# Moving convolution operations between the blocks of a spilled round in a two-layer MLP kernel

## The chip, the cores and the metric

The kernel runs on one core of one Trainium2 chip. The metric is the device time of that core in microseconds (us), from runs on the chip. A profile of one execution stands beside the times: it names the engines PE (TensorE matmuls), PEld (TensorE weight loads), DVE (VectorE), ACT (ScalarE), POOL (GpSimd) and SP (SyncE, which here only issues DMAs).

## What is computed

The reference takes x of shape (8, 4096, 192), that is 32768 tokens of width 192. A causal convolution of 7 taps runs along each sequence; the taps are a softmax over `weight`, one set for each of 8 groups of channels. Then a two-layer MLP follows: h = x @ w_in with 2048 hidden units, g = s * relu(h)^2 + b, and out = g @ w_out, with 192 outputs.

```python
out = np.einsum('hk,bskhg->bshg', w, x_unf)      # 7 taps, w = softmax(weight)
h = x @ w_in
r = np.maximum(h, 0.0)
g = s * (r * r) + b
return (g @ w_out).astype(np.float32)
```

## The kernel before

**Tokens and steps.** The 32768 tokens are 32 super-blocks of 1024, each of two blocks of 512. A block has 8 steps, one for each pair of 128-wide slices of the hidden layer (`NPAIR` = 8). A step computes its pair's hidden values on PE (`first`, line 545), applies relu and square on ACT (lines 573 and 581), splits the square into a high and a low part on DVE (line 583 makes `qh`, line 587 makes `ql`), and two steps later adds the pair's share to the output rows 0 to 127 on PE (`second`, line 763). These output rows are the "A" part.

**Rounds.** The other 64 output rows, the "B" part, are not summed step by step. The squares `q` are kept, and from the third super-block on they are summed in rounds of 48 steps, that is of six blocks (`ROUNDS`). SBUF has a ring of 12 tiles for kept squares (`RING`, `room_for`), each of two steps, so a round's last three blocks stay on the chip and its first three are written to DRAM (`send`, line 602) and read back (`call_back`, line 612, 1 MB a tile, four tiles a block). `blocks(k)` returns these two lists as `near` and `far_off`. This text calls the near blocks n0, n1, n2 and the far ones f0, f1, f2; `batch` sums them in this order, in the second step of the next round. There are ten rounds: nine are summed by `batch`, the last by `last_batch`, which the change does not touch.

**A block's sum and its eviction.** `second_B` (line 782) adds a block's eight pairs into two PSUM tiles, `acc1` and `acc2`; `banks()` takes them from the pool `ps_o`, which has two buffers of each name. So a block's sum can begin when the block two places ahead of it has been evicted: f0 waits for n1, f1 for n2, f2 for f0. `evict_B` is one ACT activation (line 795) and three DVE operations (line 799), which together combine the four quarters into an output tile, and then a DMA (line 800).

**Convolution.** The convolution of the tokens to come runs on DVE in small pieces, drawn from one stream (`pieces`): seven tap operations a block (line 194 the first, line 196 the others), then a cast on ACT (line 232), a subtraction on DVE (line 225) and two DMAs that swap halves (lines 208 and 209). `convolve(k)` draws up to k pieces and puts them where it is called; it stops when a block has its seven taps, or when the stream says "gated", which means that it is as far ahead as it may be. In `batch`, `WINDOW` = 5 pieces are drawn for each block.

**Order.** DVE, ACT, PE and SP each carry out their instructions in the order in which the program writes them (`in_order`). A piece of convolution that is written ahead of an eviction therefore runs ahead of it, on DVE and, for the cast, on ACT. Some transfers written inside a round's sums are held (`put_off`) and released together by `let_go`, after the eviction of f1. `meanwhile` in `batch` is the relu, square and split of the round's first two steps.

Of the kernel before, what the change touches and what calls it, by code (L numbers as in the profile page):

```python
# [33 lines left out]
WINDOW = 5  # L34
# [13 lines left out]
def conv_attention_then_squared_relu_mlp(  # L48
# [78 lines left out]
    @contextmanager  # L127
    def in_order(*engines):

        traced = nc.cur_bb.bb.instructions  # L130
        start = len(traced)
        yield
        for e in engines:
            mine = [i for i in traced[start:] if i.engine == e.engine]
            for before, i in zip(mine, mine[1:]):
                tc.add_manual_dep(
                    i,
                    before.name,
                    mybir.DependencyInfo(
                        mybir.DependencyClass.NoSync, mybir.DependencyReason.DATA  # L140
                    ),
                    reason="in_order",
                )
# [4 lines left out]
    def put_off(transfer):  # L148
        if holding[0]:
            later.append(transfer)  # L150
        else:
            transfer()

    def let_go():
        holding[0] = False
        for transfer in later[-1:] + later[:-1]:
            transfer()
        later.clear()
# [435 lines left out]
    def place(block):  # L594
        return block // 2, block % 2
# [12 lines left out]
    def call_back(block):  # L608

        for k in range(NPAIR // 2):  # L610
            room = room_for(F32)
            nc.sync.dma_start(room.rearrange("p a b c -> p (a b c)"), away[block][:, k])
            for i in range(2):
                kept[*place(block), 2 * k + i] = room[:, i]
        del away[block]
# [5 lines left out]
    def blocks(k):  # L621

        z = (16 * OLD + sum(ROUNDS[: k + 1])) // NPAIR
        y = z - 2 * RING // NPAIR
        return list(range(y, z)), list(range(z - ROUNDS[k] // NPAIR, y))
# [18 lines left out]
    def banks():  # L644
        return [ps_o.tile([P, BLK], F32, name=f"acc{k}") for k in (1, 2)]
# [9 lines left out]
    def out_tile(name):  # L655
        return outs[:, room.index(name), :]
# [119 lines left out]
    def second_B(n, j, accs):  # L776

        for p in range(NPAIR):
            q = kept.pop((n, j, p))
            for r in (slice(0, HB), slice(HB, P)):  # L780
                for i in range(2):
                    nc.tensor.matmul(  # L782
                        accs[r.start // HB][i * DB : (i + 1) * DB], WB[r, p, i, :], q[r, i, :],
                        start=p == 0, stop=p == NPAIR - 1, skip_group_check=True,
                    )
        return accs
# [3 lines left out]
    def evict_B(n, j, accs):  # L790

        t0 = n * SUP + j * BLK
        oB = out_tile(("oB", "oB2", "oC", "oC2", "oA", "oA2")[turn[0] % 6])[0:DB]
        turn[0] += 1
        nc.scalar.activation(  # L795
            oB, accs[0][DB:P], AF.Identity, scale=sb[DB:P], bias=bias[DB:P, 1:2]
        )
        for a in (accs[0][0:DB], accs[1][0:DB], accs[1][DB:P]):
            nc.vector.scalar_tensor_tensor(oB, a, sb[0:DB], oB, op0=ALU.mult, op1=ALU.add)  # L799
        put_off(lambda: nc.sync.dma_start(outT[P:D, t0 : t0 + BLK], oB))  # L800
# [80 lines left out]
    def convolve(k):  # L881

        k += owed[0]
        owed[0] = 0
        while k > 0:
            said = next(stream, "over")
            if said in ("over", "gated"):
                return
            k -= 1
            burst[0] = k > 0  # L890
            if said == "tapped":
                owed[0] = k
                return
# [43 lines left out]
    def batch(k, meanwhile):  # L937

        near, far_off = blocks(k)
        inputs[0] = nc.sync  # L940
        with in_order(nc.sync):
            call_back(far_off[0])
            turn[0] = 0
            for block in near + far_off:
                a = second_B(*place(block), banks())
                if block == near[0]:
                    evict_B(*place(block), a)
                    meanwhile()
                    for away_block in far_off[1:]:
                        call_back(away_block)  # L950
                convolve(WINDOW)
                if block != near[0]:
                    evict_B(*place(block), a)
                if block == far_off[-2]:
                    let_go()
            convolve(0)
        inputs[0] = nc.scalar
# [28 lines left out]
    def step(n, j, p):  # L986
# [18 lines left out]
        if edge == 1:  # L1005
            second(*queue.pop(0))

            def puts():
                *at, before = waiting.pop()
                put(*at, squares(before, nc.vector.tensor_copy))  # L1010
                put(n, j, p, squares(h, nc.vector.tensor_copy))

            batch(k - 1, puts)
            return
# [89 lines left out]
```

## Time and profile before

| what | value |
|---|---|
| median of 3 runs (2245.11, 2246.98, 2247.1) | 2246.98 us |
| time of the profiled execution | 2247.28 us |
| its span, from the first instruction to the last | 2245.5 us |
| PE busy | 2220.7 us (99%) |
| PEld busy | 1612.3 us (72%) |
| DVE busy | 1668.6 us (74%) |
| ACT busy | 1297.8 us (58%) |
| mean granted TensorE clock | 0.999 of full speed |

The execution lasts 1.78 us longer than its span. Busy time is the share in which an engine has an instruction running; PE's is pipelined, and an end of a matmul is modelled, so the time that PE loses is better read from the starts of its instructions. A wait in the profile names the instruction that came last before a waiting one could start.

### The profile page before, as it was taken

How to read it: one execution, taken by the hardware profiler on the slowest of the kernel's cores; microseconds unless marked ns; L12 is line 12 of the kernel's file. 1: busy time of each engine (PE TensorE's matmuls, PEld its weight loads, DVE VectorE, ACT ScalarE, POOL GpSimd, SP SyncE). 2: the span in 40 equal slices, each digit the busy share in tenths (PEclk: the TensorE clock that was granted, in tenths of full speed). 3: DMA queues.
4: the chain of work that ended last, by engine and by line, in shares of the span. 5: the costliest groups of instructions: out<-in, count | busy, mean ns of one | idle time of the engine just before them, and what ended most of it. 6: DMA issues, size and time to landing. Idle time of an engine off the chain costs nothing.

```text
span 2245.5 us, 44788 instructions
## 1 busy us (share of the span) xinstructions
PE 2220.7 (99%) x19334; PEld 1612.3 (72%) x19334; DVE 1668.6 (74%) x2036; ACT 1297.8 (58%) x1390; POOL 108.9 (5%) x81
## 2 busy tenths in 40 slices
PE   9999999999999999999999999999999999999999
PEld 6788874886688478848865885788488748856884
DVE  8888876787678768867876787678668667876863
ACT  8758653664467356626653663566266536644662
POOL 0011000000000000000000000000000000000000
PEclk9999999999999999999999999999999999999999
DMA  5116427524551554185336525541753275245506
GB/s 165 38 36 231 134 76 290 202 72 167 217 199 52 240 184 147 53 313 179 104 122 235 202 72 236 190 157 53 266 186 135 77 290 202 71 181 216 181 20 244
DMA packets 75846, 361.43 MB, mean 161 GB/s; under 512 B 10624, under 2 KB 10880, under 8 KB 44928
## 3 DMA queue, kind: packets, MB, share of 16 engines
q1 hardware_dynamic: 68160, 337.07, 41.2%
q10 hardware_dynamic: 7488, 21.50, 3.3%
q8 instruction: 151, 2.47, 0.4%
q14 instruction: 47, 0.39, 0.1%
HBM read 157.47 MB, written 150.99 MB: 137 GB/s over the span
## 4 chain that ended last, share of the span: by engine, by line
PE 97%; DVE 2%; ACT 0%; DMA 0%; issue 0%; SPq 0%; DVEq 0%; ACTq 0%
PE h L545 46%; PE acc L763 29%; PE acc L782 17%; PE h L782 2%; PE acc L709 2%; DVE outs L799 1%; PE acc L679 0%; ACT outs L795 0%; PE acc L685 0%; PE acc L687 0%; DVE acc L196 0%; PE acc L686 0%; DVE ql L587 0%; PE acc L678 0%; DMA xA<-in_xA 0%; PE acc L681 0%
## 5 line engine op out<-in xcount | busy, mean ns | idle before, releaser
L573 ACT ACTIVATE q<-h 128x1024 f32<-128x1024 f32 x512 | 525.9, 1027 | 514.1 <-PE h L545 504.3
L587 DVE TENSOR_TENSOR ql<-q,qh 128x1024 fp32r<-128x1024 f32 x498 | 610.9, 1227 | 55.1 <-ACT qh L583 5.0
L763 PE MATMUL acc<-qh,W 64*128 64x512 f32 x3816 | 587.9, 386 | 0.0
L583 DVE CAST qh<-q 128x1024 fp32r<-128x1024 f32 x482 | 333.9, 693 | 329.7 <-ACT q L581 326.8
L581 ACT ACTIVATE q<-q 128x1024 f32<-128x1024 f32 x512 | 543.6, 1062 | 16.0
L545 PE MATMUL h<-wB,W 64*128 64x512 f32 x1536 | 430.0, 386 | 0.0
L545 PE MATMUL h<-sB,W 64*128 64x512 f32 x1536 | 430.0, 386 | 0.0
L545 PE MATMUL h<-sA,W 64*128 64x512 f32 x3024 | 426.0, 387 | 0.0
L545 PE MATMUL h<-wA,W 64*128 64x512 f32 x3024 | 424.8, 386 | 0.0
L782 PE MATMUL acc<-q,WB 64*64 64x512 f32 x3520 | 393.3, 593 | 19.6 <-DVE outs L799 19.6
L763 PEld LDWEIGHTS acc<-qh,W 64*128 64x128 f32 x3816 | 357.5, 184 | 75.7 <-issue 0.8
L763 PE MATMUL acc<-ql,W 64*128 64x512 f32 x1908 | 371.5, 386 | 0.0
L782 PEld LDWEIGHTS acc<-q,WB 64*64 64x64 f32 x3520 | 134.8, 133 | 272.8 <-issue 237.1
L545 PEld LDWEIGHTS h<-sA,W 64*128 64x128 f32 x3024 | 282.4, 184 | 66.6 <-PE acc L782 7.3
L545 PEld LDWEIGHTS h<-wA,W 64*128 64x128 f32 x3024 | 283.3, 184 | 59.6
L545 PEld LDWEIGHTS h<-sB,W 64*128 64x128 f32 x1536 | 282.6, 184 | 30.7 <-issue 0.2
L545 PEld LDWEIGHTS h<-wB,W 64*128 64x128 f32 x1536 | 282.6, 184 | 30.2
L196 DVE SCALAR_TENSOR_TENSOR acc<-xA,tap,acc 128x512 f32<-128x512 f32 x378 | 292.2, 773 | 6.3
L799 DVE SCALAR_TENSOR_TENSOR outs<-acc,sb,outs 64x512 f32<-64x512 f32 x165 | 123.1, 746 | 131.8 <-ACT outs L795 123.3
L763 PEld LDWEIGHTS acc<-ql,W 64*128 64x128 f32 x1908 | 178.6, 184 | 37.6
L795 ACT ACTIVATE outs<-acc,bias,sb 64x512 f32<-64x512 f32 x55 | 42.6, 774 | 258.6 <-PE acc L782 258.4
L772 POOL TENSOR_TENSOR outs<-outs 128x512 f32<-128x512 f32 x59 | 95.2, 1613 | 1768.9 <-ACT outs L771 1768.9
(141 smaller groups left out, 857.7 us busy)
## 6 DMA issues: line engine op xcount, KB each, us to landing
away<-q SPq DMA_DIRECT2D x120, 1024.0 KB, 5.8
q<-away SPq DMA_DIRECT2D x120, 1024.0 KB, 10.0
wA<-sA SPq DMA_DIRECT2D x124, 256.0 KB, 3.7
wB<-sB SPq DMA_DIRECT2D x62, 256.0 KB, 4.0
outT<-outs SPq DMA_DIRECT2D x59, 256.0 KB, 2.1
xA<-in_xA ACTq DMA_DIRECT2D x23, 515.0 KB, 3.6
outT<-outs SPq DMA_DIRECT2D x62, 128.0 KB, 3.4
xB<-in_xB ACTq DMA_DIRECT2D x21, 259.0 KB, 2.8
```

Of the source, the lines that this page charges most:

```text
L196: nc.vector.scalar_tensor_tensor(acc, src, w[:, k : k + 1], acc, op0=ALU.mult, op1=ALU.add)
L545: nc.tensor.matmul(h[:, i, :], w_in(w, p, chunk[0], rows), chunk[part], start=start, stop=stop)
L573: nc.scalar.activation(q, h, AF.Relu)
L581: nc.scalar.activation(q, q, AF.Square)
L583: cast(qh, q)
L587: nc.vector.tensor_tensor(ql, q, qh.bitcast(F32), op=ALU.subtract)
L709: nc.tensor.matmul(accs[to + 2 * i][0:cols], w(f, r), q[r, f % 2, :], start=start and f == 0, stop=stop and f == NF - 1,)
L763: nc.tensor.matmul(accs[i], w(f, r), q[r, f % 2, :], start=f == 0 and lo == 0, stop=f == ends[i] and lo == 2,)
L772: nc.gpsimd.tensor_tensor(o, o, o2, op=ALU.add)
L782: nc.tensor.matmul(accs[r.start // HB][i * DB : (i + 1) * DB], WB[r, p, i, :], q[r, i, :], start=p == 0, stop=p == NPAIR - 1, skip_group_c ...
L795: nc.scalar.activation(oB, accs[0][DB:P], AF.Identity, scale=sb[DB:P], bias=bias[DB:P, 1:2])
L799: nc.vector.scalar_tensor_tensor(oB, a, sb[0:DB], oB, op0=ALU.mult, op1=ALU.add)
```

## The change

In `batch`, the five pieces of convolution of n0 and of n1 are no longer drawn. The other four blocks draw their five pieces ahead of their evictions, as they did.

```diff
             for block in near + far_off:
                 a = second_B(*place(block), banks())
+                if block not in near[:2]:
+                    convolve(WINDOW)
+                evict_B(*place(block), a)
                 if block == near[0]:
-                    evict_B(*place(block), a)
                     meanwhile()
                     for away_block in far_off[1:]:
                         call_back(away_block)
-                convolve(WINDOW)
-                if block != near[0]:
-                    evict_B(*place(block), a)
                 if block == far_off[-2]:
                     let_go()
             convolve(0)
```

**DVE, from the end of `meanwhile` to the eviction of f0, first round.** A DVE eviction is one row with `acc1` and one row x2 with `acc2`. Before, where acc_3863 and acc_3864 belong to n1, acc_3910 and acc_3911 to n2, acc_3951 and acc_3952 to f0:

```order
L587 TENSOR_TENSOR ql<-q,qh 128x1024
L196 SCALAR_TENSOR_TENSOR acc<-xB,tap,acc 128x512 x4
L194 TENSOR_SCALAR acc<-xA,tap 128x512
L225 TENSOR_TENSOR sB<-acc,sB 128x512
L196 SCALAR_TENSOR_TENSOR acc<-xA,tap,acc 128x512 x3
L799 SCALAR_TENSOR_TENSOR outs<-acc_3863,sb,outs 64x512
L799 SCALAR_TENSOR_TENSOR outs<-acc_3864,sb,outs 64x512 x2
L196 SCALAR_TENSOR_TENSOR acc<-xA,tap,acc 128x512 x3
L799 SCALAR_TENSOR_TENSOR outs<-acc_3910,sb,outs 64x512
L799 SCALAR_TENSOR_TENSOR outs<-acc_3911,sb,outs 64x512 x2
L194 TENSOR_SCALAR acc<-xA,tap 128x512
L196 SCALAR_TENSOR_TENSOR acc<-xA,tap,acc 128x512 x6
```

Now, where acc_3859 and acc_3860 belong to n1, acc_3897 and acc_3898 to n2, acc_3939 and acc_3940 to f0:

```order
L587 TENSOR_TENSOR ql<-q,qh 128x1024
L799 SCALAR_TENSOR_TENSOR outs<-acc_3859,sb,outs 64x512
L799 SCALAR_TENSOR_TENSOR outs<-acc_3860,sb,outs 64x512 x2
L196 SCALAR_TENSOR_TENSOR acc<-xB,tap,acc 128x512 x4
L799 SCALAR_TENSOR_TENSOR outs<-acc_3897,sb,outs 64x512
L799 SCALAR_TENSOR_TENSOR outs<-acc_3898,sb,outs 64x512 x2
L194 TENSOR_SCALAR acc<-xA,tap 128x512
L225 TENSOR_TENSOR sB<-acc,sB 128x512
L196 SCALAR_TENSOR_TENSOR acc<-xA,tap,acc 128x512 x3
L799 SCALAR_TENSOR_TENSOR outs<-acc_3939,sb,outs 64x512
L799 SCALAR_TENSOR_TENSOR outs<-acc_3940,sb,outs 64x512 x2
L196 SCALAR_TENSOR_TENSOR acc<-xA,tap,acc 128x512 x3
```

Nine DVE operations that stood between `meanwhile` and the eviction of n1 now stand behind it: four behind n1's eviction, five behind n2's.

**DVE, the end of the round's sums, first round.** Now, from the eviction of f1 (acc_3986, acc_3987) to that of f2 (acc_4038, acc_4039) and the split of the next step:

```order
L799 SCALAR_TENSOR_TENSOR outs<-acc_3986,sb,outs 64x512
L799 SCALAR_TENSOR_TENSOR outs<-acc_3987,sb,outs 64x512 x2
L194 TENSOR_SCALAR acc<-xA,tap 128x512
L196 SCALAR_TENSOR_TENSOR acc<-xA,tap,acc 128x512 x6
L799 SCALAR_TENSOR_TENSOR outs<-acc_4038,sb,outs 64x512
L799 SCALAR_TENSOR_TENSOR outs<-acc_4039,sb,outs 64x512 x2
L583 CAST qh<-q 128x1024
```

The seven tap operations of the last convolution block stood ahead of f0's eviction before, and the evictions of f1 and f2 had no convolution ahead of them. The number of DVE operations in a round is the same: what was not drawn for n0 and n1 is drawn for f1 and f2, which drew nothing before because the stream was already gated.

**ACT, the same place, first round.** The difference, with the cast of the convolution's block (`sB`) and the first operations of the evictions of n1 to f2:

```order
 L581 ACTIVATE q<-q 128x1024
-L232 CAST sB<-acc 128x512
-L795 ACTIVATE outs<-acc_3863,bias,sb 64x512
-L795 ACTIVATE outs<-acc_3910,bias,sb 64x512
-L795 ACTIVATE outs<-acc_3951,bias,sb 64x512
-L795 ACTIVATE outs<-acc_3997,bias,sb 64x512
-L795 ACTIVATE outs<-acc_4046,bias,sb 64x512
+L795 ACTIVATE outs<-acc_3859,bias,sb 64x512
+L795 ACTIVATE outs<-acc_3897,bias,sb 64x512
+L232 CAST sB<-acc 128x512
+L795 ACTIVATE outs<-acc_3939,bias,sb 64x512
+L795 ACTIVATE outs<-acc_3986,bias,sb 64x512
+L795 ACTIVATE outs<-acc_4038,bias,sb 64x512
```

The cast moved from ahead of n1's eviction to ahead of f0's. On PE no instruction moves. On SP, the load of the next `xB` and the two swaps of `sB`, which are held until `let_go`, now stand behind the output DMAs of n2 and f0 instead of ahead of them.

## Rows read from the trace of the kernel before

**Rows 1.** The page: busy time, and the chain that ended last by engine.

```profile
PE 2220.7 (99%) x19334; PEld 1612.3 (72%) x19334; DVE 1668.6 (74%) x2036; ACT 1297.8 (58%) x1390; POOL 108.9 (5%) x81
...
PE 97%; DVE 2%; ACT 0%; DMA 0%; issue 0%; SPq 0%; DVEq 0%; ACTq 0%
```

**Rows 2.** Waits: waiting engine and line, releaser: total us, times, longest us.

```profile
PE acc L782 <- DVE outs L799: 19.6, 18, 1.6
...
PE acc L410 <- POOL xA L180: 1.0, 1, 1.0
```

**Rows 3.** Timeline of PE, second round's sums: start us, us, instruction, [idle before].

```profile
537.99 20.83 PE L782 MATMUL acc<-q,WB 64*64 64x512 f32 x192
560.44 1.08 PE L782 MATMUL acc<-q,WB 64*64 64x512 f32 x4 [1.62 <-DVE outs L799]
562.07 20.82 PE L782 MATMUL acc<-q,WB 64*64 64x512 f32 x188 [0.56 <-DVE outs L799]
582.82 0.96 PE L545 MATMUL h<-sA,W 64*128 64x512 f32 x6
```

**Rows 4.** Stretches of the first, second, last round's sums: us, busy PE to POOL, PEclk, DMA.

```profile
328.02:374.54 46.52, 44.34 (x386) 15.10 (x384) 29.43 (x40) 10.59 (x13) 1.27 (x1) 0.96 0.76 303
537.99:582.82 44.83, 42.66 (x387) 14.66 (x385) 29.43 (x40) 10.60 (x13) 1.27 (x1) 1.00 0.80 315
...
2195.95:2237.32 41.37, 41.37 (x388) 14.60 (x386) 14.00 (x18) 5.95 (x7) 0.00 (x0) 1.00 0.80 321
```

**Rows 5.** Stretches just behind the stall, first and second round, same columns.

```profile
352.10:356.40 4.30, 4.30 (x24) 1.41 (x28) 4.06 (x6) 0.00 (x0) 0.00 (x0) 0.60 1.01 427
562.10:566.40 4.30, 4.30 (x40) 1.55 (x44) 4.06 (x6) 0.00 (x0) 0.00 (x0) 1.00 1.01 429
```

**Rows 6.** Timeline of DVE, second round's sums.

```profile
551.75 1.23 DVE L587 TENSOR_TENSOR ql<-q,qh 128x1024 fp32r<-128x1024 f32 x1
552.89 3.11 DVE L196 SCALAR_TENSOR_TENSOR acc<-xB,tap,acc 128x512 f32<-128x512 f32 x4
555.91 0.48 DVE L194 TENSOR_SCALAR acc<-xA,tap 128x512 f32<-128x512 f32 x1
556.68 0.69 DVE L225 TENSOR_TENSOR sB<-acc,sB 128x512 fp32r<-128x512 f32 x1 [0.29 <-ACT sB L232]
557.29 2.32 DVE L196 SCALAR_TENSOR_TENSOR acc<-xA,tap,acc 128x512 f32<-128x512 f32 x3
559.64 2.38 DVE L799 SCALAR_TENSOR_TENSOR outs<-acc,sb,outs 64x512 f32<-64x512 f32 x3
...
567.09 4.69 DVE L196 SCALAR_TENSOR_TENSOR acc<-xA,tap,acc 128x512 f32<-128x512 f32 x6
...
582.92 2.38 DVE L799 SCALAR_TENSOR_TENSOR outs<-acc,sb,outs 64x512 f32<-64x512 f32 x3 [4.44 <-ACT outs L795]
```

**Rows 7.** Timeline of ACT, second round's sums: evictions of n0, n1, n2.

```profile
545.12 0.78 ACT L795 ACTIVATE outs<-acc,bias,sb 64x512 f32<-64x512 f32 x1 [5.62 <-PE acc L782]
...
556.03 0.62 ACT L232 CAST sB<-acc 128x512 fp32r<-128x512 f32 x1 [5.04 <-DVE acc L196]
556.67 0.77 ACT L795 ACTIVATE outs<-acc,bias,sb 64x512 f32<-64x512 f32 x1
```

**Rows 8.** Reads back from DRAM, second round: issues 5, 9 and 12, us to landing.

```profile
L612 SPq DMA_DIRECT2D q<-away x1: 319/319/319, 548.6 to 548.6; - x1
...
DMA to landing us min/median/max: 7.8/7.8/7.8
...
L612 SPq DMA_DIRECT2D q<-away x1: 320/320/320, 555.5 to 555.5; - x1
DMA to landing us min/median/max: 11.7/11.7/11.7
...
L612 SPq DMA_DIRECT2D q<-away x1: 319/319/319, 564.0 to 564.0; - x1
DMA to landing us min/median/max: 11.0/11.0/11.0
```

**Rows 9.** Timeline after the second round's sums: DVE's next split, PE's next A sums.

```profile
585.00 0.62 PE L763 MATMUL acc<-qh,W 64*128 64x512 f32 x4
...
587.35 0.69 DVE L583 CAST qh<-q 128x1024 fp32r<-128x1024 f32 x1 [2.06 <-ACT q L581]
...
588.08 1.23 DVE L587 TENSOR_TENSOR ql<-q,qh 128x1024 fp32r<-128x1024 f32 x1
...
591.80 0.62 PE L763 MATMUL acc<-qh,W 64*128 64x512 f32 x4
```

## The prediction

> **What bounds the kernel now.** I read the page first. PE is busy for 99% of the span, and the chain of work that ended last is 97% PE and 2% DVE [rows 1]. So only two things can change the time: what PE has to do, which this edit leaves alone, and the moments in which PE stands still. The list of waits shows these moments. PE waits for the second part of an eviction, DVE's line 799, 18 times and 19.6 us in all [rows 2]: twice in each of the nine rounds that `batch` sums. The next wait of PE in the same list is 1.0 us, once, at the start [rows 2].
>
> Next I read PE's timeline in one round [rows 3]. The reader is to see that n0, n1 and n2 run as one unbroken group of 192 matmuls, that f0 begins only at 560.44, gets four matmuls out, and stands still again until 562.07. The idle times in brackets, 1.62 and 0.56 us, are measured from modelled ends of matmuls and understate the loss. A stretch says it better: a round's sums take 44.83 us from their first matmul to the next step's first, and the last round's, which are the same 384 matmuls with no wait, take 41.37 us [rows 4]. The loss is 44.83 - 41.37 = 3.46 us a round.
>
> The first round loses more: 46.52 us [rows 4]. In the stretch right behind its stall the granted clock is 0.60 on the mean and PE gets 24 matmuls out, where the second round has 1.00 and 40 [rows 5]. Part of that stretch ran at the lower of the clock's two levels, 1.2 instead of 2.4 GHz, after PE had stood still. That costs 46.52 - 44.83 = 1.69 us, once in this execution.
>
> **Why f0 waits.** It needs n1's two PSUM tiles. A block takes 41.37 / 6 = 6.90 us, so n1's sum, which began 6.90 us into the round, ends at 537.99 + 13.79 = 551.78. Its eviction has two parts, and both are late. On ACT the first part starts at 556.67, behind the cast of the convolution's block, for which ACT itself idled 5.04 us until DVE had the taps done [rows 7]. On DVE the rest starts at 559.64, behind nine convolution operations that began at 552.89 [rows 6]. PE would have begun f0 at 537.99 + 3 x 6.90 = 558.68.
>
> **The change, part by part.** All times are worked out for the second round, with durations from rows 3 to 7.
>
> *n1's eviction moves ahead of nine DVE operations and of the cast.* After n0's sum, which ends at 544.89, ACT started its part at 545.12 [rows 7], 0.23 us later, and needs 0.78 us. For n1 that gives ACT 552.0 to 552.8. DVE is free at 551.75 + 1.23 = 552.98, so its three operations run to 552.98 + 2.38 = 555.4. f0 may begin at 558.68: 3.3 us to spare. The whole stall of 3.46 us goes, and with it, on this reading, the clock's drop behind it.
>
> *The nine operations stand elsewhere.* The four xB taps (3.11 us) run from 555.4 to 558.5, while PE is still on n2. n2's sum ends at 558.68; ACT takes its part to 559.7, DVE to 562.1. f1 needs these tiles at 565.57: 3.5 us to spare. Then come one xA tap, the subtraction and three taps, 0.48 + 0.69 + 2.32 = 3.5 us, to 565.6; the cast that the subtraction needs stands behind n2's eviction on ACT and ends by 560.4. f0's sum ends at 565.57, its eviction at about 569.0, and f2 needs the tiles at 572.47: 3.5 us again. Three more taps (2.3 us) end at 571.3, ahead of f1's eviction, which ends at about 575.9. The next A sums take f1's tiles; they start 2.18 us behind the round's sums [rows 3, 9], at 581.5, so 5.6 us are to spare. No PE wait takes the old one's place.
>
> *Seven taps move to the end.* One of 0.48 and six in 4.69 us [rows 6] run from 575.9 to 581.1, and f2's eviction from there to 583.5. PE ends f2 at 579.36, so DVE is done 4.1 us behind the sums; before it was 582.92 + 2.38 - 582.82 = 2.5 us. DVE's next work, a split, came 4.5 us behind the sums [rows 3, 9], when ACT had its input. So the taps cost nothing here, with 0.4 us in hand. Were that gone, the split's result, ready at 589.31, is first needed by the A sums at 591.80 [rows 9]: 2.5 us more.
>
> *Transfers.* f1 and f2 begin 3.46 us earlier, and their squares are read back from DRAM at a DMA share of 1.01 [rows 5], so this must be looked at. The fifth read, f1's first, lands at 548.6 + 7.8 = 556.4, and f1 needs it at 565.57. The ninth, f2's first, lands at 555.5 + 11.7 = 567.2 and is needed at 572.47. The twelfth lands at 564.0 + 11.0 = 575.0 and is needed, as f2's seventh pair, 5.17 us into f2, at 577.6 [rows 8]. The margins are 9, 5.3 and 2.6 us. The reads are issued as tiles come free, and PE frees f0's first tile earlier than before, so they land no later. SP's held transfers (the xB load and the sB swaps) now stand behind two more output DMAs, and the squares' writes to DRAM, queued behind f2's output, are issued about 1.6 us later against the end of the sums. What the held ones bring is first needed many steps of 3.4 us each later (line 763's rows at 585.00 and 591.80 are two steps apart [rows 9]). I put all this at nothing.
>
> *Sum.* 9 x 3.46 = 31.1 us, plus 1.69 us for the clock: 32.8 us. The profiled execution took 2247.28 us, so 2247.28 - 32.8 = **2214.5 us**. That execution lies 0.3 us above the median of 2246.98. The fastest run shown, 2245.11, lies 2.2 us below it, about the price of the clock's drop; without a drop its sum would be 2245.11 - 31.1 = 2214.0. Both ways give the same. Bounds of what I do not know: if the drop is not tied to the stall and stays, 2216.2; if one wait of up to 0.5 us a round is left, 4.5 us more, 2219.0. I see no row for a larger gain: the next listed wait of PE is 1.0 us [rows 2], and the last round's 41.37 us is what the matmuls take.
>
> **A rule that speaks against it.** PE's three near blocks run without a gap on two pairs of tiles [rows 3], and the last round, which spreads over other tiles too, has none at all [rows 4]. The Trainium skill (Perfetto Trace Analysis, Identifying Performance Opportunities) reads the same gap repeated on the engine that should be full as a possible sign of too little PSUM for the next tile. By that reading the order of DVE's work would change nothing and the sum would stay at 2247.3. That is the first rival.
>
> **The rivals.**
> *The stall moves.* With only two pairs of tiles, a wait of PE could turn up at f1 or f2, where convolution now stands ahead of the eviction. Price 3.46 us a round, so 2247 us, or about 2230 if half of it moves. Against it: an eviction with nothing ahead of it takes 0.23 + 0.78 + 2.38 = 3.4 us of a block's 6.90, and the convolution that stands ahead of n2's, f0's and f1's evictions (3.1, 3.5 and 2.3 us) fits into the rest of the block before, which is 3.5 us. The fit at f0 is close: if DVE were late by a whole 3.5 us there, PE would wait. For it: the pieces are drawn by a rule that looks at no clock.
>
> *DVE's tail makes PE wait (the slower side).* The seven taps ahead of f2's eviction delay the split of the next step, and with it the A sums at what is 591.80 before. It decides from 0.4 + 2.5 = 2.9 us of further delay on DVE; the time is 2214.5 + 9 x (delay - 2.9). To be slower than before, the delay must pass 2.9 + 3.46 = 6.4 us; at 7 us it is 2251. Against it: DVE is idle for part of this stretch (29.43 us busy of 44.83 [rows 4]), and the seven taps have all their inputs long before.
>
> *The reads from DRAM bind.* f2 would wait for its last tile. It decides from 2.6 us of lateness; at 4 us of lateness the round loses 1.4 us, and the time is 2214.5 + 9 x 1.4 = 2227. Against it: the reads run back to back before, whatever PE does.
>
> *The change doesn't do what it says.* Were the pieces drawn somewhere else, outside the sums, DVE would have the work in the steps, where it waits for ACT anyway. The orders in the section on the change show them inside the sums, in the same number. No chance of its own.
>
> **How the numbers follow.** A difference under 0.2%, 4.5 us, can't be told from no change. Forecast, all nine stalls gone: 0.86, with 2212.5 to 2219 as its own range (0.5 us a round above, the offset of the profiled run and a little more below). Part of a stall left, moved, or DRAM: 0.07, 2220 to 2240, still faster. The whole stall moves: 0.04, same. DVE's tail: 0.03, slower. The forecast alone holds over eight in ten, so the range is 2212.5 to 2219. Faster 0.93, same 0.04, slower 0.03.
>
> **What would show it.** In the profile after: no wait of PE's line 782 for line 799; a round's sums 41.4 us from first matmul to next step; ACT's first part of n1's eviction 0.2 us behind n1's sum, with the cast behind n2's; line 799 of n1 ending some 3 us before f0's first matmul; a granted clock of 1.00 throughout. I am wrong if a round's sums stay near 44.8 us, if PE waits for a read of `away`, or if line 763 waits for `ql` after a round.

## The result, and the profile after

The changed kernel takes 2214.28 us, median of 4 runs from 2214.01 to 2214.52, against 2246.84 us before, median of 4 runs from 2245.11 to 2247.10. The ratio is 0.9857, with a 95% interval of 0.9840 to 0.9874: 1.4% faster. The forecast was 2214.5 us.

The page of the kernel after, the lines that answer to [rows 1]:

```profile
span 2212.6 us, 44771 instructions
...
PE 2207.9 (100%) x19334; PEld 1611.5 (73%) x19334; DVE 1668.1 (75%) x2036; ACT 1297.9 (59%) x1390; POOL 109.3 (5%) x81
...
PE 98%; DVE 1%; DMA 1%; ACT 0%; SPq 0%; issue 0%; DVEq 0%; ACTq 0%
```

PE has the same 19334 matmuls and DVE the same 2036 operations. DVE's busy time has hardly moved (1668.6 before). Nothing was saved in work; the span lost 32.9 us because PE stands still less.

The list of waits of the kernel after. The 18 waits of PE for evictions [rows 2] are gone, and the only wait of PE's matmuls left in the list is the one at the start:

```profile
PE acc L410 <- POOL xA L180: 1.0, 1, 1.0
```

Stretches of the first, the second and the last round's sums, with the columns of [rows 4]:

```profile
327.76:369.12 41.36, 41.36 (x387) 14.59 (x385) 27.82 (x38) 9.89 (x12) 1.27 (x1) 1.00 0.84 335
532.59:573.95 41.36, 41.36 (x388) 14.59 (x386) 27.47 (x38) 9.89 (x12) 1.27 (x1) 1.00 0.83 333
2163.03:2204.40 41.37, 41.37 (x387) 14.60 (x386) 14.00 (x18) 5.95 (x7) 0.00 (x0) 1.00 0.80 321
```

The reader is to see that the rounds summed in `batch` now take what the last round takes, 41.36 us, with PE busy for all of it and a granted clock of 1.00 in the first round too. A round took 44.83 us, the first 46.52 [rows 4]. So 44.83 - 41.36 = 3.47 us a round, 31.2 us in nine rounds, and 1.69 us of lower clock: 32.9 us, which is the whole difference of the spans.

Where the eviction of n1 went, in the timeline of DVE, second round:

```profile
546.34 1.23 DVE L587 TENSOR_TENSOR ql<-q,qh 128x1024 fp32r<-128x1024 f32 x1
547.60 2.38 DVE L799 SCALAR_TENSOR_TENSOR outs<-acc,sb,outs 64x512 f32<-64x512 f32 x3
549.89 3.10 DVE L196 SCALAR_TENSOR_TENSOR acc<-xB,tap,acc 128x512 f32<-128x512 f32 x4
554.26 2.38 DVE L799 SCALAR_TENSOR_TENSOR outs<-acc,sb,outs 64x512 f32<-64x512 f32 x3 [1.26 <-ACT outs L795]
556.56 0.47 DVE L194 TENSOR_SCALAR acc<-xA,tap 128x512 f32<-128x512 f32 x1
556.95 0.68 DVE L225 TENSOR_TENSOR sB<-acc,sB 128x512 fp32r<-128x512 f32 x1
557.55 2.32 DVE L196 SCALAR_TENSOR_TENSOR acc<-xA,tap,acc 128x512 f32<-128x512 f32 x3
561.12 2.38 DVE L799 SCALAR_TENSOR_TENSOR outs<-acc,sb,outs 64x512 f32<-64x512 f32 x3 [1.26 <-ACT outs L795]
...
575.92 2.38 DVE L799 SCALAR_TENSOR_TENSOR outs<-acc,sb,outs 64x512 f32<-64x512 f32 x3
578.50 0.69 DVE L583 CAST qh<-q 128x1024 fp32r<-128x1024 f32 x1 [0.20 <-ACT q L581]
```

The round begins at 532.59, so f0 begins at 532.59 + 41.36 / 2 = 553.27. n1's eviction is over at 549.98, 3.3 us earlier; before, line 799 started at 559.64, after f0 was due [rows 6]. f2 is due at 567.06, and f0's eviction, which began at 561.12, is over at 563.5. Behind the sums DVE had 0.20 us of idle time left ahead of the next split. In this the second round stands alone: in the other eight the trace has 0.55 or 0.56 us there.

ACT's parts of the evictions of n1, n2 and f0, and the cast, in the timeline of ACT, second round:

```profile
546.58 0.77 ACT L795 ACTIVATE outs<-acc,bias,sb 64x512 f32<-64x512 f32 x1 [1.01 <-PE acc L782]
553.45 0.77 ACT L795 ACTIVATE outs<-acc,bias,sb 64x512 f32<-64x512 f32 x1 [6.09 <-PE acc L782]
554.25 0.62 ACT L232 CAST sB<-acc 128x512 fp32r<-128x512 f32 x1
560.32 0.77 ACT L795 ACTIVATE outs<-acc,bias,sb 64x512 f32<-64x512 f32 x1 [5.45 <-PE acc L782]
```

n1's sum ends at 532.59 + 41.36 / 3 = 546.38, so its part starts 0.2 us behind it, and the cast stands behind n2's, as the prediction said.

### The profile page after: what moved, and what is told of

The parts are those of the page before. It is cut to its first block, busy times and chain, and to the rows that moved or that the text cites. A ratio compares the mean times of both kernels' runs of the same rounds, so it can differ in the third digit from the quotient of the medians.

```text
span 2212.6 us, 44771 instructions
## 1 busy us (share of the span) xinstructions
PE 2207.9 (100%) x19334; PEld 1611.5 (73%) x19334; DVE 1668.1 (75%) x2036; ACT 1297.9 (59%) x1390; POOL 109.3 (5%) x81
## 4 chain that ended last, share of the span: by engine, by line
PE 98%; DVE 1%; DMA 1%; ACT 0%; SPq 0%; issue 0%; DVEq 0%; ACTq 0%
PE h L545 47%; PE acc L763 29%; PE acc L782 17%; PE h L782 2%; PE acc L709 2%; DMA q<-in_w 0%; PE acc L679 0%; PE acc L685 0%; PE acc L687 0%; DVE acc L196 0%; PE acc L686 0%; DVE ql L587 0%; PE acc L678 0%; PE acc L681 0%; DMA xA<-in_xA 0%; DVE qh L583 0%
## 5 line engine op out<-in xcount | busy, mean ns | idle before, releaser
L782 PE MATMUL acc<-q,WB 64*64 64x512 f32 x3520 | 380.0, 590 | 0.0
```

The lines of the kernel that those rows point to most:

```text
L782: nc.tensor.matmul(accs[r.start // HB][i * DB : (i + 1) * DB], WB[r, p, i, :], q[r, i, :], start=p == 0, stop=p == NPAIR - 1, skip_group_c ...
```

## The experiments

Theory: f0 waits for n1's tiles, these wait for the DVE part of n1's eviction, and DVE works through its queue in order; PE pays only what passes the room that each eviction has. The rivals: the ACT part behind the cast is what holds the tiles; two pairs of tiles are too few whatever the order; every operation ahead of an eviction is paid. Each ratio below is to runs of the kernel before that were made beside the experiment: 13 for the first four (median 2246.84 us) and 7 others for the last two (median 2247.88 us).

**How much room is there: only n0's pieces left out.**

```diff
-                if block not in near[:2]:
+                if block not in near[:1]:
```

> Only n0's pieces are left out; n1 draws its pieces ahead of its eviction again, which come to the four xB taps (3.1 us on DVE) and no cast on ACT. In the changed kernel n1's eviction ends 3.3 us before f0 could use its tiles. Theory (PE waits only if the eviction ends later than f0's first matmul): 3.1 us fit into 3.3 us, so no wait or one of up to 0.2 us a round, 2214 to 2216 us, sums of a round 41.4 to 41.6 us. Rival (every operation ahead of n1's eviction is paid by PE): 9 x 3.1 = 28 us more, 2242 us.

Measured: 2214.5 us (2214.40 to 2214.63), ratio to the kernel before 0.9858 (0.9844 to 0.9873). The timelines of DVE and of PE, second round:

```profile
547.75 3.11 DVE L196 SCALAR_TENSOR_TENSOR acc<-xB,tap,acc 128x512 f32<-128x512 f32 x4
550.88 2.38 DVE L799 SCALAR_TENSOR_TENSOR outs<-acc,sb,outs 64x512 f32<-64x512 f32 x3
```

```profile
532.85 41.43 PE L782 MATMUL acc<-q,WB 64*64 64x512 f32 x384
```

The eviction ends at 553.26; f0 is due at 532.85 + 20.68 = 553.53. Four taps ahead of the eviction cost PE nothing: all 384 matmuls are one unbroken group. So it is not true that every operation ahead of an eviction is paid, and leaving out n1's pieces as well gains nothing that can be measured. Half of the change would have done.

**The edge of the room: two operations more.** The experiment before, and this ahead of n1's eviction; the operations rework a tile of column sums that nothing needs any more.

```diff
+                if block == near[1]:
+                    extra(2)
                 evict_B(*place(block), a)
...
+    def extra(n):
+        spare = sumA.rearrange("p a b -> p (a b)")
+        for _ in range(n):
+            nc.vector.scalar_tensor_tensor(
+                spare, spare, tapA[:, 0:1], spare, op0=ALU.mult, op1=ALU.add
+            )
```

> As the kernel with only n0's pieces left out, and two more DVE operations of about 0.75 us (on a tile that nothing needs any more) ahead of n1's eviction. Theory: the 3.3 us of room are used up by the four taps, so 1.2 us of the added 1.5 us, or a little less because the second tile is needed 0.4 us after the first, reach PE in each of nine rounds: 2221 to 2226 us, waits of PE's line 782 for the eviction back, longest about 1 us. Rival (there is more room than the timeline shows): 2214 to 2216 us. Should the clock drop behind one of these waits, 1 to 2 us more.

Measured: 2225.86 us (2225.75 to 2226.35), at the upper end of what was expected; ratio 0.9909 (0.9892 to 0.9925). Timelines of DVE and of PE, then the stretch of the second round's sums:

```profile
552.04 1.53 DVE L940 SCALAR_TENSOR_TENSOR sumA<-sumA,tap 128x512 f32<-128x512 f32 x2
553.61 2.38 DVE L799 SCALAR_TENSOR_TENSOR outs<-acc,sb,outs 64x512 f32<-64x512 f32 x3
```

```profile
534.12 21.68 PE L782 MATMUL acc<-q,WB 64*64 64x512 f32 x196
556.04 20.82 PE L782 MATMUL acc<-q,WB 64*64 64x512 f32 x188 [0.24 <-DVE outs L799]
```

```profile
534.12:576.79 42.67, 42.43 (x387) 14.74 (x385) 30.76 (x42) 10.61 (x13) 1.27 (x1) 1.00 0.80 322
```

PE gets f0's first four matmuls out, then waits until the eviction is over at 555.99. The waits of PE's line 782 for the eviction are back, but far shorter in the list than the 1 us that was expected:

```profile
PE acc L782 <- DVE outs L799: 2.2, 9, 0.2
```

The stretch tells what they cost. A round loses 42.67 - 41.36 = 1.31 us, and nine lose 11.8 us; the time is 11.6 us over the changed kernel's. The same wait in the same place, made by operations of no use, is the mechanism shown from the other side. The edge lies where the timeline puts it.

**Is it the cast on ACT: the ACT part alone moved.** The kernel before, with n1's pieces drawn between the ACT part and the DVE part of its eviction.

```diff
-    def evict_B(n, j, accs):
+    def evict_B(n, j, accs, between=None):
...
+        if between:
+            between()
         for a in (accs[0][0:DB], accs[1][0:DB], accs[1][DB:P]):
...
+                if block == near[1]:
+                    evict_B(*place(block), a, lambda: convolve(WINDOW))
+                else:
+                    convolve(WINDOW)
+                    if block != near[0]:
+                        evict_B(*place(block), a)
```

> The kernel before, with the ACT part of n1's eviction moved ahead of n1's pieces, so that it no longer stands behind the cast; the DVE part stays behind the nine operations. Theory (the DVE queue alone sets when n1's tiles come free): ACT's part starts near 552 instead of 556.7 in the second round, line 799 of n1 still near 559.6, sums of a round 44.8 us, 2245 to 2247 us. Rival (the cast ahead of it on ACT is what holds the eviction): the wait goes, 2214 to 2220 us.

Measured: 2246.51 us (2244.92 to 2249.07), ratio 1.0000 (0.9991 to 1.0009). Timeline of ACT, then of DVE, then of PE, second round, then stretches of the first, second and third round's sums:

```profile
550.18 0.77 ACT L795 ACTIVATE outs<-acc,bias,sb 64x512 f32<-64x512 f32 x1 [1.03 <-PE acc L782]
554.20 0.62 ACT L232 CAST sB<-acc 128x512 fp32r<-128x512 f32 x1 [3.24 <-DVE acc L196]
```

```profile
555.46 2.32 DVE L196 SCALAR_TENSOR_TENSOR acc<-xA,tap,acc 128x512 f32<-128x512 f32 x3
557.81 2.38 DVE L801 SCALAR_TENSOR_TENSOR outs<-acc,sb,outs 64x512 f32<-64x512 f32 x3
```

```profile
558.66 1.07 PE L782 MATMUL acc<-q,WB 64*64 64x512 f32 x4 [1.67 <-ACT outs L795]
560.24 22.51 PE L782 MATMUL acc<-q,WB 64*64 64x512 f32 x188 [0.51 <-DVE outs L801]
```

```profile
327.90:372.73 44.83, 42.65 (x386) 14.69 (x384) 29.43 (x40) 10.61 (x13) 1.27 (x1) 1.00 0.79 314
536.16:582.69 46.53, 44.35 (x387) 15.18 (x386) 29.43 (x40) 10.61 (x13) 1.27 (x1) 0.96 0.76 303
746.12:792.22 46.10, 44.10 (x386) 14.54 (x385) 29.43 (x40) 10.61 (x13) 1.27 (x1) 0.96 0.77 305
```

ACT's part of n1's eviction now starts at 550.18, with the cast behind it, and is done 6.9 us before the DVE part starts. It gains nothing. f0 starts at 558.66, 0.1 us after the end of the first of the three DVE operations, which began at 557.81 and takes about 0.75 us. The bracket on PE's row names ACT's line 795 for this wait. That line's part for n1 was over at 550.95, so the name is misleading here; the timeline of DVE tells who was late. The cast on ACT was late too, but it was not what PE waited for.

**Is it the number of tiles: a third pair for f0.** The kernel before, convolution where it was.

```diff
-                a = second_B(*place(block), banks())
+                if block == far_off[0]:
+                    h = ps_h.tile([P, 2, BLK], F32, name="h")
+                    a = [h[:, k, :] for k in range(2)]
+                else:
+                    a = banks()
+                a = second_B(*place(block), a)
```

> The kernel before, all convolution where it was, but f0 sums into a pair of tiles of the pool of the hidden values, which are idle in a round's sums, instead of into n1's. Theory (PE waits for tiles, and the order of DVE's work matters only through them): f0 starts with no wait, f1 finds n1's tiles evicted near 562 when it needs them at 565.6, f2 n2's; sums of a round 41.4 us, 2214 to 2216 us. Rival (DVE is late as such, and another block or the next step waits instead): 2225 to 2247 us.

Measured: 2214.35 us (2214.15 to 2214.52), ratio 0.9858 (0.9843 to 0.9872). Timeline of PE and of DVE, second round:

```profile
532.69 20.83 PE L782 MATMUL acc<-q,WB 64*64 64x512 f32 x192
553.34 7.05 PE L782 MATMUL h<-q,WB 64*64 64x512 f32 x64
560.21 13.91 PE L782 MATMUL acc<-q,WB 64*64 64x512 f32 x128
```

```profile
554.35 2.38 DVE L799 SCALAR_TENSOR_TENSOR outs<-acc,sb,outs 64x512 f32<-64x512 f32 x3
```

DVE is as late with n1's eviction as before: it starts at 554.35, 1.0 us after f0 has begun. It makes no difference now, because f0 does not want those tiles. So PE's wait was for tiles and for nothing else, and there are two ways to end it, an earlier eviction or another pair of tiles. They come out equal: with either, the sums run as fast as the matmuls go, and nothing is left for the two together.

**The tail: six operations behind f2's eviction.** The changed kernel, and at the end of the sums:

```diff
+            extra(6)
             convolve(0)
```

> The changed kernel with six more DVE operations of about 0.75 us (on a tile that nothing needs any more) at the end of each round's sums, behind f2's eviction and ahead of the split of the next step. Theory (the tail costs only what passes 0.2 us of idle time ahead of that split and 2.5 us from its end to the A sums that need it): 4.5 - 2.7 = 1.8 us a round at most, a little less because the high part is needed before the low one, so 2226 to 2231 us, with waits of PE's line 763 for DVE's lines 583 and 587. Rival (the tail has room for all of it): 2214 to 2216 us. Rival (each operation is paid): 9 x 4.5 = 41 us, 2255 us.

Measured: 2225.47 us (2225.31 to 2225.60), 0.5 us below what was expected; ratio 0.9901 (0.9885 to 0.9918). Timeline of DVE, then of PE, behind the second round's sums:

```profile
579.23 4.67 DVE L940 SCALAR_TENSOR_TENSOR sumA<-sumA,tap 128x512 f32<-128x512 f32 x6
583.82 0.69 DVE L583 CAST qh<-q 128x1024 fp32r<-128x1024 f32 x1
584.54 1.23 DVE L587 TENSOR_TENSOR ql<-q,qh 128x1024 fp32r<-128x1024 f32 x1
```

```profile
585.82 0.50 PE L763 MATMUL acc<-ql,W 64*128 64x512 f32 x2 [0.53 <-DVE ql L587]
```

The sums themselves are untouched; PE waits in the steps behind them, where the prediction put it. 11.2 us in nine rounds are 1.24 us a round for 4.6 us of added work, so the tail's room is about 3.4 us. The expectation had counted on the second round's 0.20 us of idle time; with the 0.55 us of the other rounds it would have come out lower.

**The fit at f0: nine operations ahead of its eviction.** The changed kernel, and `extra(9)` ahead of f0's eviction, as above.

> The changed kernel with nine more DVE operations of about 0.75 us (6.8 us) ahead of f0's eviction, where the prediction called the fit close. In the changed kernel DVE idles 1.26 us ahead of that eviction, and the eviction ends 3.5 us before f2 could use the tiles. Theory: 6.8 - 1.26 - 3.5 = 2.0 us of lateness reach PE each round, at f2 and nowhere else, so 2230 to 2234 us, sums of a round about 43.4 us. Rival (the fit is closer than that, as the prediction reckoned, with no idle time ahead of the eviction): 3.3 us a round, 2243 to 2246 us. A drop of the clock behind one of these waits would add 1 to 2 us.

Measured: 2235.19 us (2234.95 to 2235.44), 1.2 us above the theory's range and far below the rival's; ratio 0.9945 (0.9930 to 0.9960). Timeline of DVE, then of PE, second round:

```profile
561.75 7.04 DVE L940 SCALAR_TENSOR_TENSOR sumA<-sumA,tap 128x512 f32<-128x512 f32 x9
568.83 2.38 DVE L799 SCALAR_TENSOR_TENSOR outs<-acc,sb,outs 64x512 f32<-64x512 f32 x3
```

```profile
534.55 34.56 PE L782 MATMUL acc<-q,WB 64*64 64x512 f32 x320
569.62 1.08 PE L782 MATMUL acc<-q,WB 64*64 64x512 f32 x4 [0.51 <-DVE outs L799]
571.26 7.08 PE L782 MATMUL acc<-q,WB 64*64 64x512 f32 x60 [0.56 <-DVE outs L799]
578.27 0.96 PE L545 MATMUL h<-sA,W 64*128 64x512 f32 x6
```

Five blocks of 64 matmuls run unbroken and f2 waits, as it should: the wait stands at whichever block's tiles are late. A round takes 578.27 - 534.55 = 43.72 us and loses 2.36. f2 is due at 534.55 + 34.47 = 569.02, and the eviction is over at 571.21, 2.2 us later. The theory had 2.0: it counted 6.8 us for the nine operations, which took 568.83 - 561.75 = 7.08. The rest of the miss is about 0.15 us a round.

## Why the prediction was right

*What bounds the kernel.* A round's loss was read as the difference of two stretches [rows 4] and not as the idle time in brackets. The brackets give 2.18 us a round [rows 3], 19.6 in all; the stretches give 3.46, and 3.47 is what came back. By the list of waits alone the forecast would have been 11.6 us too small. Most of what the brackets leave out is the 1.08 us of f0's first four matmuls [rows 3]: they count as busy, but PE starts them two at a time where an unbroken stretch starts four (last section).

*n1's eviction.* Forecast to be over 3.3 us before f0; it was. That the wait falls, and moves nowhere, followed from each block's room, and the two experiments at the edge (four taps free, two operations more paid) show that the room is what decides.

*ACT and DVE.* "Both are late" was right, but the prediction left open which of them held PE. The experiment with ACT's part moved shows that it was DVE alone.

*The fit at f0.* Called close, because 3.5 us of convolution stand in 3.5 us. By the prediction's own times there was more room: the taps end at 565.6 and f0's sum at 565.57, and DVE's part of the eviction adds to what ACT's part has written, 0.23 + 0.78 = 1.0 us later. This idle time was left out. In the trace after, ACT's part starts at 560.32, and DVE idled 1.26 us until it was done, so the room is 1.26 + 3.5 = 4.8 us. That agrees with the nine operations, whose 7.08 us made the eviction 2.2 us late. The room was sized too small; it cost the forecast nothing.

*The tail.* Forecast 0.4 us of idle time and 2.5 us more, 2.9 together; there were 0.20 us of idle time in the second round and 0.55 or 0.56 in the others, and the experiment gives about 3.4 together. The place and the mechanism were right.

*The reads from DRAM.* The twelfth read of the second round in the trace after:

```profile
L612 SPq DMA_DIRECT2D q<-away x1: 319/319/319, 555.2 to 555.2; - x1
...
DMA to landing us min/median/max: 14.1/14.1/14.1
```

It lands at 569.3. f2 needs it 5.17 us after its start at 567.06, at 572.2, so 2.9 us are to spare, where 2.6 were forecast. It is issued earlier against the round's start than before, takes longer, and lands at the same point of the round (36.7 us in, 37.0 before [rows 3, 8]). No run made these reads late, so what that would cost was not tried.

*The held transfers.* Put at nothing, and no engine's wait for the load of `xB` or for the swaps of `sB` is in the list after. They stand behind two more output DMAs, as the prediction says, but these are n1's and n2's, and not n2's and f0's as the section on the change has it.

*The clock.* The 1.69 us went with the stall, and no profile of a kernel without a long stall shows such a drop. That the drop hangs on the stall is argued from profiles (last section).

*The rule of the Trainium skill* (Perfetto Trace Analysis, Identifying Performance Opportunities), that a repeated gap can mean too little PSUM, was weighed as a reason for no gain. As a diagnosis the trace agrees: a third pair of tiles ends the gap, 2214.35 us. Read as a forecast for this change it failed: two pairs are enough here, because each eviction ends before the block that needs its tiles begins.

## What to carry to other kernels

When PE waits for a PSUM tile, work out for each block when the tile is due and what stands ahead of its eviction in the evicting engine's queue: here deferrable work cost nothing up to that room, and about its length beyond. Size the loss by the starts of matmuls, or by the same stretch elsewhere without a wait, and not by the listed idle time. If reordering is hard, another pair of tiles that stands idle at that moment does the same.

## What the runs showed that was not expected

**A round loses what the second tile is late.** In an unbroken stretch PE starts its matmuls in groups of four, one group every 0.43 us: at 553.24, 553.67 and 554.09 in the changed kernel, around the start of f0. In the kernel with two operations added, PE's timeline around the same place reads:

```profile
554.34 1.45 PE L782 MATMUL acc<-q,WB 64*64 64x512 f32 x8
556.04 1.52 PE L782 MATMUL acc<-q,WB 64*64 64x512 f32 x12 [0.24 <-DVE outs L799]
```

The first row is a group of four at 554.34, the last of n2, then two matmuls at 554.77 and two at 555.20; from 556.04 on they start in fours again, until the round's last two groups, at 575.83 and 576.26, which have two each. `second_B` writes for each pair two matmuls on the first tile and two on the second, and each stands twice in the profile. So in an unbroken stretch half of a group is for the second tile, which is due together with the first, and not 0.4 us behind it, as the expectation of the experiment with two operations had it. In that experiment it was 556.04 - (534.12 + 20.68) = 1.24 us late, and the round lost 1.31. With nine operations it was 571.26 - 569.02 = 2.24 us late at f2, and the round lost 2.36. In the kernel before it was 562.07 - (537.99 + 20.68) = 3.40 us late [rows 3], and the round lost 3.47. So the loss is the lateness of the tile that comes free last, plus 0.07 to 0.12 us. The matmuls that PE gets out on the first tile meanwhile save nothing, because as many of the second tile's then run alone at the end.

**The lower clock comes behind some stalls and not others.** The profile of the kernel before shows one round of nine with a mean granted clock of 0.96 [rows 4]; that of the kernel with ACT's part moved, which has the same stall, shows two, at 46.53 and 46.10 us, and 44.83 to 44.84 in the others. Its profiled run took 2248.42 us. The runs of the kernel before fall into three groups that fit none, one and two such drops: 13 of them, made beside the first experiments, lie six at 2245.0 to 2245.6, three at 2246.8 to 2247.1, and four at 2247.9 to 2248.2. Their mean granted clocks are 1.000, 0.999 and 0.998, group by group. Seven more, made beside the last two experiments, go with the second and the third, by time and by clock. Kernels whose rounds lose 2.4 us or less show none in their profiles, and their runs lie within 0.6 us. So the change also took away most of the spread from run to run. What picks the round was not tried.
